# Running products of neighbouring groups made in shared steps, in a fused attention, MoE and FFN kernel

## The chip, the cores and the metric

The kernel runs on one core of one Trainium2 chip. The metric is the device time of one execution in microseconds (us). The kernel before took 1003.48 us (median of 3 runs, 1002.42 to 1005.08).

## The reference

Three stages follow one another; all data are float32, and the weights of the last stage come as float64 bits.

```python
# 1. attention with a decaying state: 4 batches x 8 heads, S = 768 steps, D = 48
a = a_re + i a_im, scaled by min(|a|, 0.999) / (|a| + 1e-6)
for t in range(S):
    state = a[t] * state + k[t] (x) v[t]      # complex, 48 x 48, a per row
    y[t]  = q[t] . Re(state)
# 2. mixture of 8 experts on 3072 tokens of 384 columns, one expert each
out[mask] = gate * (relu(x[mask] @ w1[e]) @ w2[e])
# 3. feed-forward: h = ((x @ w1) * (x @ w2)) @ w3 ; out = h @ w_out
```

## The kernel before

The 768 steps are cut into chunks of 64 steps, and four chunks of every batch and head make a group: three groups of 128 lanes by 64 steps. Within a chunk the recurrence is turned into matmuls by the running product P of the scaled a from the chunk's first step on: queries are multiplied by P, keys by its inverse.

**The elementwise stage** (`elementwise`, the first stream) makes 24 pieces of 8 steps, eight for each group, one group after the other. For a piece ScalarE (ACT) squares a and takes logarithm and exponential (`root`), and VectorE (DVE) scales (`norm`, L834 to L841) into a tile `cf` of coefficients, of which ACT copies one row negated (L842). `prefix` runs the complex product: each step is one multiply `pr<-cf,P` of 128x192 (L860) and one add `P<-pr` of 128x96 (L862), and each step needs the one before it. `power`, `weigh` and `keys` make the inverse weights, and the multiply `qk<-P,qkr` of 128x1536 (L892) makes a piece of weighted queries and keys, which a DMA stores to a DRAM tensor `qkd`. One call of `mix` weaves the steps of piece i with `keys` of piece i-2 and `norm` of piece i+1.

**The attention units** (`groups`, the second stream) wait until all eight pieces of their group are made. `ends` transposes the group's last products on TensorE (PE) and then, for groups 1 and 2, runs dense matmuls that nothing reads (`dense`, L964). Each group has eight units. A unit loads its keys and queries `kk` (L990, on SP's queue), turns them (`turn`, L974), makes scores, masks them on DVE (`at<-sc,mask`, L1006), makes outputs, and carries the state to the next chunk: `cb` or `cc` (L1074) and `W` or `ca` (L1075) on DVE, `L1073` on ACT. Outputs go on to the routing of the experts (rows L138 to L160).

**The product of w3 and w_out.** With the start of the third group, `side()` starts its steps: the loads `fdr` (L291, on SP), and `halves`, which turns float64 bits into pairs of float32 on DVE and ACT in 16 conversions: eight of 128x384 for w_out, eight of 128x512 for w3 (L322, L323, L324, L336, L337, L339). Once the third group's units are through, PE makes the first blocks `Wf` (L350 to L352), then the experts and the feed-forward stage run.

**What sets the order.** `drive` takes steps from the two streams by the costs that they yield; then a scheduler with a model of its own puts each engine's instructions in one fixed order. Each engine works through its list in that order, and waits where an instruction's inputs are not there.

Of the kernel before, what the change touches and what calls it, by code (L numbers as in the profile page):

```python
# [9 lines left out]
F32 = mybir.dt.float32  # L10
# [4 lines left out]
AF = mybir.ActivationFunctionType  # L15
# [607 lines left out]
D = 48  # L623
# [3 lines left out]
NPC = C // TP  # L627
NPIECE = NG * NPC
R2 = 2 * D
HD = NH * D  # L630
# [145 lines left out]
class Attn:  # L776
# [7 lines left out]
    def load_a(self, i):  # L784

        a = self.ep.tile([128, 2, 2, TP * D], F32, tag="a", name=f"a{i}", bufs=3)
        g, p = divmod(i, NPC)
        src = self.S.a[g].rearrange("r l (p e) -> p l r e", e=TP * D)
        if i:
            self.nc.sync.dma_start(a, src[p : p + 2].rearrange("n l r e -> l r n e"))  # L790
        else:
            for n in range(2):
                self.nc.sync.dma_start(a[:, :, n], src[n])
        return [a[:, :, n] for n in range(2)]

    def load_qk(self, i):
        g, p = divmod(i, NPC)
        x = self.e2.tile([128, TP, 2, D], F32, tag="qkr", name=f"qkr{i}", bufs=3)
        self.nc.sync.dma_start(x, self.S.qk[g, :, p * TP : (p + 1) * TP])
        return x  # L800

    def elementwise(self, aside, factors):
# [41 lines left out]

        def twice(c):

            p, r, d = (list(x) for x in c.ap)
            return bass.AP(tensor=c.tensor, offset=c.offset + r[0], ap=[p, [r[0], 2], [-r[0], 2], d])

        def prefix(i):  # L850
            p = i % NPC
            P[i] = e2.tile([128, TP, 2, D], F32, tag="P", name=f"P{i}", bufs=3)
            for t in range(TP):
                if p == 0 and t == 0:
                    v.tensor_copy(P[i][:, 0], cf[i][:, 0, 1:3])
                    yield 120
                    continue
                pv = P[i][:, t - 1] if t else P[i - 1][:, TP - 1]
                pr = e2.tile([128, 2, 2, D], F32, tag="pr", name=f"pr{i}_{t}", bufs=2)
                v.tensor_tensor(out=pr, in0=twice(cf[i][:, t]), in1=bc(pv, 2, 1), op=ALU.mult)  # L860
                yield 270
                v.tensor_tensor(out=P[i][:, t], in0=pr[:, :, 0], in1=pr[:, :, 1], op=ALU.add)  # L862
                yield 170

        def power(i):
            g, p = divmod(i, NPC)
            s2[i] = e2.tile([128, 2, E], F32, tag="s2", name=f"s2_{i}", bufs=2)
            act.activation(out=s2[i].rearrange("p r (t d) -> p t r d", d=D), in_=P[i], func=AF.Square)  # L868
            if p == NPC - 1:
                self.last[g] = l = self.st.tile([128, 2, 2, D], F32, tag="td", name=f"td{g}")  # L870
                act.copy(l, P[i][:, TP - 1].unsqueeze(2).to_broadcast([128, 2, 2, D]))

# [6 lines left out]
        def keys(i):  # L879
            g, p = divmod(i, NPC)  # L880
            k = raw[i][:, :, 1]
            x, g0 = s2[i][:, 0], s2[i][:, 1]
            if p == NPC - 1:
                v.tensor_copy(S.xm[:, g], px[i][:, E - D :])
            v.tensor_tensor(out=x, in0=px[i], in1=g0, op=ALU.mult)
# [7 lines left out]
            yield 1740  # L893
            dst = S.qkd[g].rearrange("q c h b (p t) w e -> p (q c h b) (t w e)", p=NPC)[p]
            self.stored = self.qk.pop(i).rearrange("p t w r d -> p (t w r d)")
            if p == NPC - 1:
                nc.sync.dma_start(dst[:64], self.stored[:64])
                done = nc.gpsimd.dma_start(dst[64:], self.stored[64:])
            else:
                done = nc.gpsimd.dma_start(dst, self.stored)  # L900
            with self.tc.issue_after(done.ins):
# [24 lines left out]
        for i in range(NPIECE + 1):  # L926
# [7 lines left out]
            if i + 1 < NPIECE:  # L934
                raw[i + 1] = self.load_qk(i + 1)
            ends = [j >= 0 and j % NPC == NPC - 1 for j in (i - 2, i - 1)]
            rest = [keys(i - 2)] if i > 1 and not ends[0] else []
# [169 lines left out]
    def groups(self, route, side, free):  # L1107
# [14 lines left out]
        yield lambda: self.made >= NPC  # L1122
# [3 lines left out]
        step = 0  # L1126
        for n, u in enumerate(work):
            g, q, c = u
            if q == 0 and c == 0:
                while self.pool and self.made < (g + 1) * NPC:  # L1130
                    yield self.fill(1)
                yield lambda: self.made >= (g + 1) * NPC
                yield from self.ends(g)
                for x in work[n : n + 2]:
                    ld[x] = self.loads(x)
                if g == NG - 1:
                    yield free
                    singles = side.fuse.units
                    side()
            self.pool.append(Item("scores", self.scores(u, ld[u][1])))  # L1140
            for x in self.chain(u, ld.pop(u)):
                yield x
                yield self.fill(S.fillcost)
                step += 1
                if g == NG - 1:
# [265 lines left out]
```

## Time and profile before

| | |
|---|---|
| median of 3 runs | 1003.48 us (1002.42 to 1005.08) |
| the profiled execution | 1001.18 us, its span 999.5 us |
| granted TensorE clock, mean over the span | 0.944 |
| busy over the span | PE 898.7 us (90%), DVE 609.1 (61%), ACT 487.3 (49%), POOL 130.9 (13%) |

The profile's page has the span in 40 slices of 25 us, a digit for the busy tenths of each, and below them the granted clock in tenths:

```profile
PE   3545899967997988999989999998999999999997
DVE  6999999997993885576489995442232323232222
PEclk9666999978997999899999999999999999999999
```

The elementwise stage is the run of nines of DVE in the slices 2 to 12. From the slice 18 on PE stands at 8 or 9 nearly throughout: there the experts and the feed-forward stage run.

### The profile page before, as it was taken

What the parts mean: (1) busy time and instruction counts of PE and PEld (TensorE: products, weight loads), DVE (VectorE), ACT (ScalarE), POOL (GpSimd) and SP (SyncE); (2) the same over time, 40 slices, a digit from 0 to 9 for tenths busy, and PEclk for the clock granted to TensorE, in tenths of its full rate; (3) what the DMA queues carried; (4) which work ended last, traced back from release to release, by engine and by line L of the source; (5) the groups of instructions that cost most, each with busy time, mean ns of one, the idle gap of its engine ahead of it and who ended that gap; (6) DMA issues with size and microseconds to landing.
All of it is one profiled execution on the core that took longest, in us unless ns stands there. A gap on an engine that the chain in (4) does not pass through costs nothing. (4 is left out here: it accounts for less than half of the span.)

```text
span 999.5 us, 17055 instructions
## 1 busy us (share of the span) xinstructions
PE 898.7 (90%) x6402; PEld 768.5 (77%) x6402; DVE 609.1 (61%) x1373; ACT 487.3 (49%) x1089; POOL 130.9 (13%) x197
## 2 busy tenths in 40 slices
PE   3545899967997988999989999998999999999997
PEld 1222478746886877989989999997888888888886
DVE  6999999997993885576489995442232323232222
ACT  6555688866774775444456654543231313121211
POOL 5111000211020211000232211110000000000001
PEclk9666999978997999899999999999999999999999
DMA  6566975448737763453677745630000000000000
GB/s 221 180 203 234 297 254 176 130 131 283 233 121 242 226 208 124 147 176 118 192 214 188 203 112 136 138 66 2 1 9 24 10 23 9 24 8 25 9 24 31
DMA packets 90183, 128.75 MB, mean 129 GB/s; under 512 B 7232, under 2 KB 72688, under 8 KB 90096
## 3 DMA queue, kind: packets, MB, share of 16 engines
q1 hardware_dynamic: 76300, 82.61, 28.9%
q0 software_dynamic: 10688, 40.36, 11.4%
q10 hardware_dynamic: 3108, 4.65, 1.7%
q8 instruction: 51, 0.84, 0.4%
q14 instruction: 36, 0.29, 0.1%
HBM read 92.38 MB, written 35.22 MB: 128 GB/s over the span
## 5 line engine op out<-in xcount | busy, mean ns | idle before, releaser
L606 DVE TENSOR_TENSOR ab<-asb,pb 128x512 f32<-128x512 f32 x48 | 33.0, 687 | 189.8 <-PE pb L352 184.2
L345 ACT CAST h<-w 128x384 fp32r<-128x384 f32 x128 | 65.1, 513 | 95.8 <-PE ph L351 50.9
L346 DVE TENSOR_TENSOR l<-w,h 128x384 fp32r<-128x384 f32 x128 | 70.6, 554 | 63.2 <-ACT h L345 60.6
L601 ACT COPY asb<-pa 128x512 f32<-128x512 f32 x48 | 28.2, 587 | 123.1 <-PE pa L352 117.0
L345 ACT CAST gh<-ab 128x512 fp32r<-128x512 f32 x48 | 29.7, 620 | 94.7 <-DVE ab L606 94.7
L816 PE MATMUL x<-s,ident 128*128 128x384 f32 x64 | 36.2, 703 | 43.5 <-ACT s L868 43.5
L351 PE MATMUL py<-hl,h 128*128 128x432 f32 x192 | 70.0, 365 | 3.5 <-DVE hl L407 3.5
L350 PE MATMUL py<-hh,h 128*128 128x432 f32 x192 | 69.2, 361 | 0.8 <-ACT hh L406 0.8
L350 PE MATMUL ph<-xh,h 128*128 128x432 f32 x192 | 69.7, 364 | 0.0
L352 PE MATMUL ph<-xh,l 128*128 128x432 f32 x192 | 69.6, 363 | 0.0
L351 PE MATMUL ph<-xl,h 128*128 128x432 f32 x192 | 69.6, 362 | 0.0
L352 PE MATMUL py<-hh,l 128*128 128x432 f32 x192 | 69.1, 360 | 0.0
L860 DVE TENSOR_TENSOR pr<-cf,P 128x192 f32<-128x192 f32 x189 | 66.6, 353 | 3.3
L974 PE MATMUL tr<-ident,kk 128*96 128x128 f32 x384 | 60.1, 289 | 9.1 <-DMA kk<-qkd 8.4
L351 PE MATMUL po<-ol,gh 128*128 128x384 f32 x192 | 65.0, 338 | 0.0
L350 PE MATMUL po<-oh,gh 128*128 128x384 f32 x192 | 64.8, 338 | 0.0
L352 PE MATMUL po<-oh,gl 128*128 128x384 f32 x192 | 64.2, 338 | 0.0
L570 POOL DMA_INDIRECT out<-ob,mdp x24 | 23.8, 992 | 307.6 <-DVE ob L569 165.8
L975 ACT COPY qkT<-tr 96x512 f32<-96x512 f32 x96 | 54.7, 591 | 18.2 <-PE tr L974 17.7
L350 PE MATMUL pa<-yh,ah 128*128 128x512 f32 x144 | 57.5, 399 | 3.0 <-ACT yh L345 3.0
L816 PEld LDWEIGHTS x<-s,ident 128*128 128x128 f32 x64 | 14.9, 258 | 56.7 <-ACT s L868 49.3
L350 PE MATMUL pb<-yh,bh 128*128 128x512 f32 x144 | 57.3, 398 | 0.0
(218 smaller groups left out, 2400.5 us busy)
## 6 DMA issues: line engine op xcount, KB each, us to landing
w<-in_w SPq DMA_DIRECT2D x128, 192.0 KB, 2.7
kk<-qkd SPq DMA_DIRECT2D x24, 768.0 KB, 9.7
qkd<-qk POOLq DMA_DIRECT2D x21, 768.0 KB, 5.7
qkr<-in_qk SPq DMA_DIRECT2D x24, 384.0 KB, 4.1
a<-in_a SPq DMA_DIRECT2D x11, 768.0 KB, 5.4
fdr<-in_w SPq DMA_DIRECT2D x16, 512.0 KB, 5.2
fdr<-in_v POOLq DMA_DIRECT2D x12, 512.0 KB, 6.5
xs<-zr POOLq DMA_DIRECT2D x8, 648.0 KB, 7.6
```

The lines of the kernel that those rows point to most:

```text
L345: nc.scalar.copy(H, src)
L346: nc.vector.tensor_tensor(out=L, in0=src, in1=H.bitcast(F32), op=ALU.subtract)
L350: nc.tensor.matmul(out, lh, rh, start=first, stop=False)
L351: nc.tensor.matmul(out, lh, rl, start=False, stop=False)
L352: return nc.tensor.matmul(out, ll, rh, start=False, stop=last)
L570: nc.gpsimd.indirect_dma_start(out=S.outv[j], out_offset=bass.IndirectOffsetOnAxis(ap=S.mdp[:, j, 0:1], axis=0), in_=ob, in_offset=None, b ...
L601: nc.scalar.copy(asb, pa)
L606: nc.vector.tensor_tensor(out=ab, in0=asb, in1=pb, op=ALU.mult)
L816: nc.tensor.matmul(p, S.ident, s[r], start=r == 0, stop=r == 1)
L860: v.tensor_tensor(out=pr, in0=twice(cf[i][:, t]), in1=bc(pv, 2, 1), op=ALU.mult)
L974: nc.tensor.transpose(pt[:, h], qk[:, h0 + h, w], self.S.ident)
L975: nc.scalar.copy(qkT[:, w, h0 : h0 + 4], pt)
```

## The change

The 24 pieces are made in 24 rounds of a new table `PAIRS`: four rounds of eight steps of group 1, eight rounds that take four steps of group 1 and four of group 2, eight rounds of groups 2 and 3 in the same way, and four rounds of group 3. In a shared round one multiply of 128x384 (L891 of the changed kernel) and one add of 128x192 (L893) make a step of both groups. `LAST` says after which round a group is complete: rounds 12, 20 and 24 instead of 8, 16 and 24. `cf` has a fourth row, which ACT copies. Loads of a and of queries and keys, and the stores, go in two parts in a shared round. `ends` calls `dense` for the first group alone. The next group's first `kk` are loaded as soon as that group is made, and `side()` starts as soon as the elementwise stage has been issued.

```diff
+HEAD = 4
+def rounds():
+    got = [((0, TP * r, TP),) for r in range(HEAD)]
+    for g in range(NG - 1):
+        more = C - HEAD * TP
+        got += [((g, HEAD * TP + t, TP // 2), (g + 1, t, TP // 2)) for t in range(0, more, TP // 2)]
+        got += [((g + 1, t, TP),) for t in range(more, C if g == NG - 2 else HEAD * TP, TP)]
+    return got
+PAIRS = rounds()
+LAST = {g: max(r for r, x in enumerate(PAIRS) if g in [y[0] for y in x]) for g in range(NG)}
...
-            cf[i] = c = ep.tile([128, TP, 3, D], F32, tag="cf", name=f"cf{i}", bufs=2)
+            cf[i] = c = ep.tile([128, TP, 4, D], F32, tag="cf", name=f"cf{i}", bufs=2)
-            v.tensor_tensor(out=c[:, :, 1:3], in0=ar, in1=bc(td(u), 2, 2), op=ALU.mult)
-            act.activation(out=c[:, :, 0], in_=c[:, :, 2], func=AF.Copy, scale=-1.0)
+            v.tensor_tensor(out=c[:, :, 0:3:2], in0=ar, in1=bc(td(u), 2, 2), op=ALU.mult)
+            act.activation(out=c[:, :, 1], in_=c[:, :, 2], func=AF.Copy, scale=-1.0)
+            act.copy(c[:, :, 3], c[:, :, 0])
...
-                v.tensor_tensor(out=pr, in0=twice(cf[i][:, t]), in1=bc(pv, 2, 1), op=ALU.mult)
-                yield 270
-                v.tensor_tensor(out=P[i][:, t], in0=pr[:, :, 0], in1=pr[:, :, 1], op=ALU.add)
-                yield 170
+                pr = e2.tile([128, 2, 2, 2, D], F32, tag="pr", name=f"pr{i}_{t}", bufs=1)[:, :j]
+                cx = c[:, :j, t].rearrange("p m (w r) d -> p m w r d", w=2)
+                v.tensor_tensor(out=pr, in0=cx, in1=bc(pv, 2, 2), op=ALU.mult)
+                yield 100 + 170 * j
+                v.tensor_tensor(out=o[:, :j, t], in0=pr[:, :, :, 0], in1=pr[:, :, :, 1], op=ALU.add)
+                yield 70 + 100 * j
...
-        if g < NG - 1:
+        if not g:
             self.dense(self.stored[:, :512], WARM)
...
-                    ld[x] = self.loads(x)
+                    if x not in ld:
+                        ld[x] = self.loads(x)
                 if g == NG - 1:
                     yield free
-                    singles = side.fuse.units
-                    side()
+            if free() and not singles:
+                singles = side.fuse.units
+                side()
...
-                if x[0] == g and x not in ld:
+                if self.made > LAST[x[0]] and x not in ld:
                     ld[x] = self.loads(x)
```

DVE in the fifth piece, before: the steps of group 1's running product, one multiply and one add each (L837 belongs to the next piece).

```order
L860 TENSOR_TENSOR pr_0_420<-cf_384,P_362 128x192
L837 SCALAR_TENSOR_TENSOR sq_351<-sq_351,y_356 128x384
L862 TENSOR_TENSOR P_419<-pr_0_420 128x96
L860 TENSOR_TENSOR pr_1_425<-cf_384,P_419 128x192
L862 TENSOR_TENSOR P_419<-pr_1_425 128x96
L860 TENSOR_TENSOR pr_2_431<-cf_384,P_419 128x192
L862 TENSOR_TENSOR P_419<-pr_2_431 128x96
L860 TENSOR_TENSOR pr_3_439<-cf_384,P_419 128x192
L862 TENSOR_TENSOR P_419<-pr_3_439 128x96
```

The same place on DVE in the changed kernel, the first shared round (its first step is group 1's alone, as group 2's first product is a copy; L860 is here the line that was L837):

```order
L891 TENSOR_TENSOR pr_0_438<-cf_398,P_376 128x192
L893 TENSOR_TENSOR P_435<-pr_0_438 128x96
L891 TENSOR_TENSOR pr_1_443<-cf_398,P_435 128x384
L893 TENSOR_TENSOR P_435<-pr_1_443 128x2x96
L891 TENSOR_TENSOR pr_2_452<-cf_398,P_435 128x384
L860 SCALAR_TENSOR_TENSOR sq_364<-sq_364,y_369 128x384
L893 TENSOR_TENSOR P_435<-pr_2_452 128x2x96
L891 TENSOR_TENSOR pr_3_460<-cf_398,P_435 128x384
L893 TENSOR_TENSOR P_435<-pr_3_460 128x2x96
```

Where eight narrow steps stood for one group, four of twice the width stand for two groups; 62 steps are of this kind.

DVE at the end of the elementwise stage, before: the last `qk` multiply, the state of group 2's last chunk (`cc`, `ca`), then the first conversion.

```order
L892 TENSOR_TENSOR qk_3533<-P_3294,qkr_3142 128x1536
L1074 TENSOR_TENSOR cc_183<-W,T_2150 96x384
L1075 TENSOR_TENSOR ca_182<-W,T_2150 96x768
L336 TENSOR_SCALAR fdm<-fdr 128x384
L337 TENSOR_SCALAR fdl<-fdr 128x384
L138 TENSOR_REDUCE mx<-lg 128x4
L339 SCALAR_TENSOR_TENSOR fdr<-fdr,fdl 128x384
```

The same place in the changed kernel, in which L923 is the `qk` multiply, L1041 the mask, L1109 and L1110 the state:

```order
L1041 TENSOR_TENSOR at_2607<-sc_2590,mask 128x512
L916 TENSOR_TENSOR s_23_2758<-s_23_2758 128x384
L918 TENSOR_TENSOR qkr_2414<-qkr_2414,s_23_2758 128x8x48
L920 SCALAR_TENSOR_TENSOR qkr_2414<-s_23_2758,qkr_2414 128x8x48
L923 TENSOR_TENSOR qk_2836<-P_2617,qkr_2414 128x1536
L1109 TENSOR_TENSOR cb_2634<-W,T_2251 96x384
L1110 TENSOR_TENSOR W<-W,T_2251 96x2x384
L1041 TENSOR_TENSOR at_2749<-sc_2732,mask 128x512
L336 TENSOR_SCALAR fdm<-fdr 128x384
L337 TENSOR_SCALAR fdl<-fdr 128x384
L339 SCALAR_TENSOR_TENSOR fdr<-fdr,fdl 128x384
```

The last `qk` multiply now has 11 of the masks of the groups 1 and 2 ahead of it instead of all 16, and the conversions begin beside group 2's fourth unit.

DVE at group 3's first mask, before (`at_3615`), which stands among the first conversions of w_out:

```order
L323 TENSOR_SCALAR fdm<-woh 128x384
L145 TENSOR_TENSOR oh_3499<-key_3492,kx_3497 128x32
L337 TENSOR_SCALAR fdl<-fdr 128x384
L324 SCALAR_TENSOR_TENSOR wol<-fdr,fdm 128x384
L160 TENSOR_TENSOR run<-run,oh_3499 128x8
L1006 TENSOR_TENSOR at_3615<-sc_3598,mask 128x512
L339 SCALAR_TENSOR_TENSOR fdr<-fdr,fdl 128x384
L1074 TENSOR_TENSOR cb_3649<-W,T_3545 96x384
```

The same mask in the changed kernel (`at_3596`), among the last conversions of w3:

```order
L1109 TENSOR_TENSOR cc_186<-W,T_2251 96x384
L1110 TENSOR_TENSOR ca_185<-W,T_2251 96x768
L324 SCALAR_TENSOR_TENSOR w3l_3762<-fdr,fdm 128x512
L322 TENSOR_TENSOR w3h_3761<-fdr,fdm 128x512
L336 TENSOR_SCALAR fdm<-fdr 128x512
L323 TENSOR_SCALAR fdm<-w3h_3761 128x512
L1041 TENSOR_TENSOR at_3596<-sc_3579,mask 128x512
L324 SCALAR_TENSOR_TENSOR w3l_3762<-fdr,fdm 128x512
L322 TENSOR_TENSOR w3h_3918<-fdr,fdm 128x512
```

Between the last `qk` multiply and group 3's first mask stand 88 of the 96 conversion instructions, four masks, five pairs of state instructions and 13 short rows of routing; before, ten conversion instructions stood there, and the others lay between the units of group 3.

## Rows read from the trace of the kernel before

**Rows 1.** Timeline of DVE: start, duration, instruction (steps of the running product).

```profile
107.62 0.36 DVE L860 TENSOR_TENSOR pr<-cf,P 128x192 f32<-128x192 f32 x1
108.01 0.26 DVE L862 TENSOR_TENSOR P<-pr 128x96 f32<-128x96 f32 x1
108.30 0.36 DVE L860 TENSOR_TENSOR pr<-cf,P 128x192 f32<-128x192 f32 x1
```

**Rows 2.** Groups of DVE by form, 0 to 305 us: busy us, mean ns | idle before.

```profile
L860 DVE TENSOR_TENSOR pr<-cf,P 128x192 f32<-128x192 f32 x189 | 66.6, 353 | 3.3
L862 DVE TENSOR_TENSOR P<-pr 128x96 f32<-128x96 f32 x189 | 47.9, 253 | 3.2
...
L834 DVE SCALAR_TENSOR_TENSOR sq<-sq,y 128x384 f32<-128x384 f32 x24 | 13.2, 549 | 0.0
L1075 DVE TENSOR_TENSOR W<-W,T 96x768 f32<-96x768 f32 x12 | 11.5, 954 | 0.0
L1006 DVE TENSOR_TENSOR at<-sc,mask 128x512 f32<-128x512 f32 x16 | 10.9, 684 | 0.9 <-PE sc L1002 0.8
```

**Rows 3.** Timeline of DVE at four places; in brackets the idle time before.

```profile
237.65 0.55 DVE L1074 TENSOR_TENSOR cb<-W,T 96x384 f32<-96x384 f32 x1 [6.69 <-ACT cb L1073]
...
303.37 1.76 DVE L892 TENSOR_TENSOR qk<-P,qkr 128x1536 f32<-128x1536 f32 x1
...
321.04 0.36 DVE L336 TENSOR_SCALAR fdm<-fdr 128x384 int32<-128x384 int32 x1 [9.63 <-DMA fdr<-in_w_out]
...
326.13 0.68 DVE L1006 TENSOR_TENSOR at<-sc,mask 128x512 f32<-128x512 f32 x1
```

**Rows 4.** Timeline of DVE: group 2's first and last mask, group 3's last.

```profile
240.16 0.69 DVE L1006 TENSOR_TENSOR at<-sc,mask 128x512 f32<-128x512 f32 x1
...
295.96 0.68 DVE L1006 TENSOR_TENSOR at<-sc,mask 128x512 f32<-128x512 f32 x1
296.56 0.24 DVE L862 TENSOR_TENSOR P<-pr 128x96 f32<-128x96 f32 x1
...
391.55 0.68 DVE L1006 TENSOR_TENSOR at<-sc,mask 128x512 f32<-128x512 f32 x1
```

**Rows 5.** Timeline of PE: the first matmul of the product of w3 and w_out.

```profile
405.57 0.69 PE L350 MATMUL Wf<-woh,w3h 128*128 128x384 f32 x1
```

**Rows 6.** Groups of ACT by form, 0 to 305 us.

```profile
L842 ACT ACTIVATE cf<-cf 128x384 f32<-128x384 f32 x24 | 12.7, 529 | 0.3
```

**Rows 7.** Timeline of SP: DMA issues.

```profile
308.99 2.53 SPq L990 DMA_DIRECT2D kk<-qkd  x3
311.69 4.62 SPq L291 DMA_DIRECT2D fdr<-in_w_out  x5
```

**Rows 8.** DMA issues, 300 to 400 us: KB each, median us to landing.

```profile
fdr<-in_w_out SPq DMA_DIRECT2D x8, 384.0 KB, 5.8
```

**Rows 9.** Waits of DVE, 100 to 410 us: us in total, times, longest.

```profile
DVE fdl L337 <- DMA fdr<-in_w: 7.9, 5, 3.7
```

**Rows 10.** Groups of DVE by line, 321 to 385 us: the conversions, and one row of routing.

```profile
L339 DVE SCALAR_TENSOR_TENSOR fdr<-fdr,fdl 128x384 f32<-128x384 uint32 (+1 forms) x16 | 9.8, 614 | 0.0
L337 DVE TENSOR_SCALAR fdl<-fdr 128x384 uint16<-128x384 uint16 (+1 forms) x16 | 6.4, 400 | 8.0 <-DMA fdr<-in_w 7.9
L336 DVE TENSOR_SCALAR fdm<-fdr 128x384 int32<-128x384 int32 (+1 forms) x16 | 6.1, 388 | 9.6 <-DMA fdr<-in_w_out 9.6
L322 DVE TENSOR_TENSOR w3h<-fdr,fdm 128x512 fp32r<-128x512 f32 x8 | 5.5, 683 | 0.0
L324 DVE SCALAR_TENSOR_TENSOR w3l<-fdr,fdm 128x512 fp32r<-128x512 f32 x8 | 5.4, 686 | 0.0
...
L324 DVE SCALAR_TENSOR_TENSOR wol<-fdr,fdm 128x384 fp32r<-128x384 f32 x8 | 4.4, 548 | 0.0
L322 DVE TENSOR_TENSOR woh<-fdr,fdm 128x384 fp32r<-128x384 f32 x8 | 4.4, 547 | 0.0
...
L323 DVE TENSOR_SCALAR fdm<-w3h 128x512 int32<-128x512 int32 x8 | 3.3, 420 | 0.0
L323 DVE TENSOR_SCALAR fdm<-woh 128x384 int32<-128x384 int32 x8 | 2.8, 355 | 0.0
...
L160 DVE TENSOR_TENSOR run<-run,oh 128x8 f32<-128x8 f32 x8 | 1.3, 158 | 0.1
```

**Rows 11.** Stretches of 25 us: busy of PE, PEld, DVE, ACT, POOL; granted clock; DMA share.

```profile
150.00:175.00 25.00, 25.00 (x330) 21.31 (x329) 23.61 (x56) 21.83 (x64) 1.06 (x2) 1.00 0.57 176
200.00:225.00 25.00, 16.84 (x94) 10.34 (x91) 24.66 (x70) 15.13 (x34) 4.07 (x5) 0.73 0.42 132
300.00:325.00 25.00, 19.79 (x180) 16.28 (x177) 9.47 (x24) 11.28 (x33) 0.57 (x1) 0.73 0.78 244
```

More of the change, by code (lines that the diff above doesn't have):

```diff
@@ L786, in load_a @@
         a = self.ep.tile([128, 2, 2, TP * D], F32, tag="a", name=f"a{i}", bufs=3)
[L787 to L794, printed above, removed]
+        at = 0
+        for g, t, n in PAIRS[i]:
+            src = self.S.a[g][:, :, t * D : (t + 2 * n) * D].rearrange("r l (m e) -> m l r e", m=2)
+            dst = a[:, :, :, at : at + n * D]
+            if i and n == TP:
+                self.nc.sync.dma_start(a, src.rearrange("m l r e -> l r m e"))
+            elif i:
+                for r in range(2):
+                    self.nc.sync.dma_start(dst[:, r], src[:, :, r].rearrange("m l e -> l m e"))
+            else:
+                for m in range(2):
+                    self.nc.sync.dma_start(dst[:, :, m], src[m])
+            at += n * D
+        return [a[:, :, m] for m in range(2)]
     def load_qk(self, i):
-        g, p = divmod(i, NPC)
         x = self.e2.tile([128, TP, 2, D], F32, tag="qkr", name=f"qkr{i}", bufs=3)
-        self.nc.sync.dma_start(x, self.S.qk[g, :, p * TP : (p + 1) * TP])
+        at = 0
+        for g, t, n in PAIRS[i]:
+            self.nc.sync.dma_start(x[:, at : at + n], self.S.qk[g, :, t : t + n])
+            at += n
         return x
@@ L843, in norm @@
+            act.activation(out=c[:, :, 1], in_=c[:, :, 2], func=AF.Copy, scale=-1.0)
+            act.copy(c[:, :, 3], c[:, :, 0])
             yield 870
-        def twice(c):
-            p, r, d = (list(x) for x in c.ap)
-            return bass.AP(tensor=c.tensor, offset=c.offset + r[0], ap=[p, [r[0], 2], [-r[0], 2], d])
         def prefix(i):
-            p = i % NPC
             P[i] = e2.tile([128, TP, 2, D], F32, tag="P", name=f"P{i}", bufs=3)
[L853 to L856, printed above, removed]
-                    continue
-                pv = P[i][:, t - 1] if t else P[i - 1][:, TP - 1]
-                pr = e2.tile([128, 2, 2, D], F32, tag="pr", name=f"pr{i}_{t}", bufs=2)
-                v.tensor_tensor(out=pr, in0=twice(cf[i][:, t]), in1=bc(pv, 2, 1), op=ALU.mult)
-                yield 270
-                v.tensor_tensor(out=P[i][:, t], in0=pr[:, :, 0], in1=pr[:, :, 1], op=ALU.add)
-                yield 170
+            m = len(PAIRS[i])
@@ new lines, in prefix @@
+            n = TP // m
+            run = lambda x: x.rearrange("p (m t) r d -> p m t r d", m=m)
+            c, o = run(cf[i]), run(P[i])
+            for t in range(n):
+                k = [k for k in range(m) if t or PAIRS[i][k][1]]
+                for x in range(m):
+                    if x not in k:
+                        v.tensor_copy(o[:, x, 0], c[:, x, 0, 0:3:2])
+                        yield 120
+                if not k:
+                    continue
+                if t:
+                    pv = o[:, :, t - 1]
+                else:
+                    old = len(PAIRS[i - 1])
+                    pv = P[i - 1].rearrange("p (m t) r d -> p m t r d", m=old)[:, old - len(k) :, TP // old - 1]
+                j = len(k)
+                pr = e2.tile([128, 2, 2, 2, D], F32, tag="pr", name=f"pr{i}_{t}", bufs=1)[:, :j]
[4 more added lines that the diff above has]
+                yield 70 + 100 * j
@@ L865, in power @@
         def power(i):
-            g, p = divmod(i, NPC)
             s2[i] = e2.tile([128, 2, E], F32, tag="s2", name=f"s2_{i}", bufs=2)
             act.activation(out=s2[i].rearrange("p r (t d) -> p t r d", d=D), in_=P[i], func=AF.Square)
-            if p == NPC - 1:
+            g, _, n = PAIRS[i][0]
+            if i == LAST[g]:
                 self.last[g] = l = self.st.tile([128, 2, 2, D], F32, tag="td", name=f"td{g}")
-                act.copy(l, P[i][:, TP - 1].unsqueeze(2).to_broadcast([128, 2, 2, D]))
+                act.copy(l, P[i][:, n - 1].unsqueeze(2).to_broadcast([128, 2, 2, D]))
@@ L893, in keys @@
             yield 1740
-            dst = S.qkd[g].rearrange("q c h b (p t) w e -> p (q c h b) (t w e)", p=NPC)[p]
             self.stored = self.qk.pop(i).rearrange("p t w r d -> p (t w r d)")
[L896 to L900, printed above, removed]
+            at = 0
+            for g, t, n in PAIRS[i]:
+                dst = S.qkd[g].rearrange("q c h b t w e -> (q c h b) t (w e)")[:, t : t + n].rearrange("l t e -> l (t e)")
+                src = self.stored[:, at * 2 * R2 : (at + n) * 2 * R2]
+                if i == LAST[g]:
+                    nc.sync.dma_start(dst[:64], src[:64])
+                    done = nc.gpsimd.dma_start(dst[64:], src[64:])
+                else:
+                    done = nc.gpsimd.dma_start(dst, src)
+                at += n
             with self.tc.issue_after(done.ins):
@@ L935, in elementwise @@
                 raw[i + 1] = self.load_qk(i + 1)
-            ends = [j >= 0 and j % NPC == NPC - 1 for j in (i - 2, i - 1)]
+            ends = [j in LAST.values() for j in (i - 2, i - 1)]
             rest = [keys(i - 2)] if i > 1 and not ends[0] else []
@@ L1126, in groups @@
         step = 0
+        singles = None
         for n, u in enumerate(work):
@@ L1144, in groups @@
                 step += 1
-                if g == NG - 1:
+                if singles:
                     for _ in range(1 + (step % 3 == 0)):
```

12 lines of the change are left out of this document (6 added, 6 removed).

## The prediction

> **What bounds the kernel now.** I read the strips of the page first. From 425 us on PE is the bound (its digits stand at 8 or 9), and the change touches nothing there; so the question is when the first matmul of the w3 and w_out product starts, 405.57 us before [rows 5]. Ahead of it I read the stretches, DVE's groups and its timeline. To 305 us DVE is full wherever the attention doesn't hold it (24.66 of 25 us at 200 to 225) [rows 11], and the running product is its largest part: 66.6 us of multiplies and 47.9 of adds [rows 2]. Its last multiply for `qkd` starts at 303.37 and ends at 305.13, and the first conversion only starts at 321.04, after 9.63 us of waiting for its load [rows 3]. PE has holes meanwhile: 16.84 busy of 25 us at 200 to 225 and 19.79 at 300 to 325, with a granted clock of 0.73 in both, between its levels of 1.2 and 2.4 GHz, against 1.00 at 150 to 175 where it is full [rows 11]. So three legs set the 405.57: DVE's elementwise work to 305, the gap and start of group 3 to its first mask at 326.13 [rows 3], and group 3, of which the last mask is at 391.55 [rows 4] and the product 14.0 us later.
>
> **The end of the elementwise work.** 62 steps now serve two groups. A 128x384 multiply costs 549 ns, as L834 does, and a 128x192 add 353, as the old multiply [rows 2]. By durations a step of two groups falls from 2 x (353 + 253) = 1212 to 902 ns; 62 of them save 19.2 us. Two bounds lie around it. Chained, with nothing between, a narrow step took 108.30 - 107.62 = 0.68 us, 0.04 more than one duration at each of its two instructions [rows 1]; a wide one would take 0.97, and 62 x (1.36 - 0.97) = 24.2. With other work between, an instruction starts about 0.08 us before its forerunner's end (the mask of 0.68 at 295.96, the add at 296.56 [rows 4]); that takes four such overlaps off 1212 and two off 902, and 62 x 0.14 = 8.7 remain. The order shows both kinds; I take 17, nearer to the durations.
>
> The Trainium skill, "VectorE: DVE Perf Modes", section "The DRAIN you can't avoid", says that the next instruction does not start until the pipe is empty. By that alone the saving would be the 19.2 of the durations; [rows 4] show a start 0.08 us ahead of the end, so the measurement decides, and the sum would move by 2 us only.
>
> Five attention units fewer stand ahead of the last `qk` multiply (11 masks in place of 16, by the order): a mask of 684, a state pair of 954 and 0.55 [rows 2, 3], less three overlaps of 0.08, make 1.93 each, 9.6 us. They are moved, not removed. The wait of 6.69 for group 2's first `cb` [rows 3], which was group 2's start in the middle of the elementwise work, has group 2 ready only at round 20 now and DVE filled with other steps; I take it as gone (bounds 0 and 6.7). 13 short routing rows at 0.158 [rows 10], with their overlaps 1.7 us in my estimate, move behind it too. So 305.1 - 17 - 9.6 - 6.7 - 1.7 = 270.1 us (262.9 with the saving at 24.2, 278.4 at 8.7).
>
> ACT gets 24 more copies of about 529 ns [rows 6], 12.7 us. In its fullest stretch it is busy for 21.83 of 25 us [rows 11]; with 12.7 us more over some 265 it rises by 1.2 a stretch, to 92%. I cost the copy at nothing: it is hidden by DVE as long as ACT is under full. Without that cover it is late for the next round's steps, at up to 0.5 us a round, 12 us.
>
> The split loads and stores cost issue time on SP and POOL alone. The dense matmuls ahead of group 2 ran in a stretch in which PE waited anyway (200 to 225 [rows 11]); without them the clock may be at 0.73 for longer at that start, but the mask rate decides below, not this start.
>
> **The gap and the conversions.** Before, the first `fdr` load was issued at 311.69, 6.6 us after the `qk` multiply's end, of which 2.53 went into issuing three loads of group 3's keys [rows 7], which aren't ahead of it now. I take 6.6 - 2.5 = 4.1 us to the issue and 5.8 to the landing [rows 8], 9.9 (bounds: 8, and the 15.9 from 305.13 to 321.04 as before [rows 3]). DVE starts to convert at 280.0.
>
> Now comes the cost. All conversions are 48.1 us of DVE (nine rows of [rows 10]: 9.8 + 6.4 + 6.1 + 5.5 + 5.4 + 4.4 + 4.4 + 3.3 + 2.8). Before, they lay among group 3's units; now 88 of 96 stand ahead of group 3's first mask. The eight left out are of the wide kind, about 0.53 each, so 43.8, less 88 overlaps of 0.08, 36.8. With four masks at 0.60 (2.4), five state pairs at 1.34 (6.7) and 13 short rows (1.3) that is 47.2 us back to back. Waits for loads come on top: 7.9 us before [rows 9], 6 taken here, since the loads have more time to run ahead (bounds 0 and 7.9). Group 3's first mask: 280.0 + 47.2 + 6 = 333.2, against 326.13 before.
>
> Group 2's five last units need 5 x 7.97 = 40 us from the last `qk` multiply on, by the pace of its masks ((295.96 - 240.16) / 7 = 7.97 [rows 4]), so PE would be ready at 318; DVE's list is what is late.
>
> **Group 3 without conversions.** Before, its eight masks took 391.55 - 326.13 = 65.4 us; group 2's took 55.8 [rows 3, 4]. I take group 2's pace, which had DVE full with other work, and the 14.0 to the product as before: 69.8 (bounds: 64, if the pace is PE's alone at about 7.1, and 79.4 as before). So the product starts at 333.2 + 69.8 = 403.0 against 405.57: 2.6 us earlier, and the rest stands as it was. From the profiled 1001.18 that is 998.6. The median of the runs lies 2.3 above the profiled execution, so 1000.9.
>
> **The rivals.**
> 1. Conversions don't hold group 3 back. They do less than I say if the steps are mostly chained (saving 24.2, end at 262.9), the load comes in 8 us and none after it is waited for: 262.9 + 8 + 47.2 = 318.1, then 69.8, product at 387.9, 17.7 us earlier. For it: every PE hole of [rows 11] disappears with the group starts. Against it: 47 us of DVE in one piece can't be shorter. Centre 12 us faster, 991 by the runs; from 5 to 22.
> 2. Slower: DVE's list between the last `qk` multiply and group 3's first mask. Its price is one us for each us that this mask comes after 405.57 - 69.8 = 335.8, and it decides from there, 2.6 us later than I forecast. With the saving at 8.7 or ACT as the bound (278.4), the load as before (15.9), waits of 7.9 and group 3's old pace: 278.4 + 15.9 + 47.2 + 7.9 + 79.4 = 428.8, 23 slower; centre 10 slower, 1013.5. For it: 88 instructions moved ahead of that mask, and each wait for a load now stops the attention too. Against it: all four bounds would have to fall on the bad side for the whole.
> 3. Small loads late: two loads of a pair become four, with rows half as long. 16 rounds held up by 1 us each would make 16 us at the elementwise end, 1015. Against it: DVE's largest waits of that time are not for loads of a, and these are issued two rounds ahead.
>
> The Trainium skill, "DMA: Bandwidth & Descriptors", section "Rules for kernel authors", wants many small transfers coalesced into one large one, which speaks against the split. No run here shows the split yet; it is what the third rival would be by that page.
>
> **How the numbers follow.** Forecast 0.46 (995 to 1007 by itself), first rival 0.27, second 0.24, third 0.03. Within 0.3%, about what a measurement of this kernel tells from no change, means 1000.5 to 1006.5. The forecast gives 0.21 faster, 0.20 same, 0.05 slower; the first rival 0.25 and 0.02 same; the second 0.03 same and 0.21 slower; the third 0.03 slower. Together 0.46, 0.25, 0.29. The range runs from 987 to 1015, which leaves the outer third of either rival out.
>
> **What would show it.** Right: multiplies of 128x384 in the steps at about 0.55 us, the last `qk` multiply ending near 270, the first conversion near 280 after a wait for `fdr`, group 3's first mask near 333 with almost no conversion after it, its masks 8 us apart, the product at 403. Wrong: a first mask at 318 or earlier (rival 1) or past 336 (rival 2), a wait of DVE for ACT's copy in the steps, ACT near full at 125 to 270, waits for a or `qkr` (rival 3), or a later part of the span that isn't the same length.

## The result and the profile after

The changed kernel took 1013.28 us (median of 4 runs, 1012.64 to 1014.76) against 1004.07 before: 1.0109 times the time before, 95% interval 1.0092 to 1.0126. It is slower, where 1000.9 us was forecast; the range of 987 to 1015 holds the time, but the sign is the second rival's. The same kernel beside the experiments gave 1.0108 (1.0075 to 1.0142). In the two profiled executions the product of w3 and w_out starts 11.4 us later (405.57 before, 416.95 now), and what follows it takes 597.8 us in place of 595.6; the account below is of the 11.4.

The steps first. In the groups of DVE to 275 us (busy us, mean ns), these answer to [rows 2]; 62 wide steps, at the durations that were taken for them:

```profile
L891 DVE TENSOR_TENSOR pr<-cf,P 128x384 f32<-128x384 f32 x62 | 34.2, 552 | 0.7
L891 DVE TENSOR_TENSOR pr<-cf,P 128x192 f32<-128x192 f32 x65 | 22.9, 353 | 1.0
L893 DVE TENSOR_TENSOR P<-pr 128x192 f32<-128x192 f32 x62 | 21.8, 352 | 0.8
```

DVE's timeline (start, duration, instruction, idle time before it) from the last `qk` multiply to group 3's last mask, with [rows 3, 4] as its counterpart:

```profile
268.58 1.76 DVE L923 TENSOR_TENSOR qk<-P,qkr 128x1536 f32<-128x1536 f32 x1
...
275.15 0.69 DVE L1041 TENSOR_TENSOR at<-sc,mask 128x512 f32<-128x512 f32 x1 [2.84 <-PE sc L1037]
280.60 0.36 DVE L336 TENSOR_SCALAR fdm<-fdr 128x384 int32<-128x384 int32 x1 [4.76 <-DMA fdr<-in_w_out]
...
282.83 0.36 DVE L336 TENSOR_SCALAR fdm<-fdr 128x384 int32<-128x384 int32 x1 [1.00 <-DMA fdr<-in_w_out]
...
284.85 0.55 DVE L1109 TENSOR_TENSOR cc<-W,T 96x384 f32<-96x384 f32 x1
...
340.00 0.68 DVE L1041 TENSOR_TENSOR at<-sc,mask 128x512 f32<-128x512 f32 x1
...
398.14 0.69 DVE L1041 TENSOR_TENSOR at<-sc,mask 128x512 f32<-128x512 f32 x1 [4.34 <-PE y L1057]
```

The elementwise stage ends at 270.3 (forecast 270.1) and the first conversion starts at 280.60 (280.0). Then it goes apart: group 3's first mask at 340.00 (333.2). The state `cc` at 284.85 stands behind nine conversion instructions, of which the first waited 4.76 us for its load and the fourth 1.00. PE's first product matmul, 405.57 before [rows 5], is at

```profile
416.95 0.69 PE L350 MATMUL Wf<-woh,w3h 128*128 128x384 f32 x1
```

ACT's timeline at the same place: the conversions have instructions there too, and the first of them waits for DVE's conversion, with group 2's state and an output copy in line behind it.

```profile
281.00 0.61 ACT L329 ACTIVATE fdm<-fdm,rebias 128x384 int32<-128x384 int32 x1 [4.22 <-DVE fdm L336]
281.55 0.55 ACT L330 ACTIVATE fdr<-fdr 128x384 f32<-128x384 f32 x1
282.00 1.60 ACT L1108 ACTIVATE cc<-W,T 96x48 f32<-96x48 f32 x8
...
284.42 0.48 ACT L1060 COPY xo<-y 128x384 f32<-128x384 f32 x1
```

And PE, which waits for that copy for 3.95 us:

```profile
284.95 0.90 PE L123 MATMUL rt<-ident,xo 128*128 128x128 f32 x3 [3.95 <-ACT xo L1060]
```

The same happens once more, without ACT between: a conversion waits 1.85 us for a load of w3, group 2's state `W` stands next but one behind it, and PE, which needs `W`, has waited 4.49 us when it gets it.

```profile
325.98 0.43 DVE L337 TENSOR_SCALAR fdl<-fdr 128x512 uint16<-128x512 uint16 x1 [1.85 <-DMA fdr<-in_w]
...
326.93 0.95 DVE L1110 TENSOR_TENSOR W<-W,T 96x768 f32<-96x768 f32 x1
```

```profile
327.94 2.87 PE L1094 MATMUL W<-cb,perm 96*96 96x384 f32 x4 [4.49 <-DVE W L1110]
```

At the other end of the attention, its beginning, I had not looked. Group 1's first mask, before and after:

```profile
123.81 0.68 DVE L1006 TENSOR_TENSOR at<-sc,mask 128x512 f32<-128x512 f32 x1
```

```profile
154.64 0.69 DVE L1041 TENSOR_TENSOR at<-sc,mask 128x512 f32<-128x512 f32 x1
```

Group 1 is complete after round 12 instead of 8, so the attention starts 30.8 us later. By group 2's first mask 8.3 of these are left (240.16 before [rows 4]):

```profile
248.43 0.68 DVE L1041 TENSOR_TENSOR at<-sc,mask 128x512 f32<-128x512 f32 x1
```

From there to group 3's first mask it takes 91.6 us (248.43 to 340.00), 86.0 before (240.16 to 326.13).

What PE does from its first `kk` transpose to the first product matmul, before and after (length, then busy PE, PEld, DVE, ACT, POOL; clock, DMA share, GB/s):

```profile
114.81:405.57 290.76, 259.56 (x3393) 211.81 (x3394) 236.49 (x600) 204.22 (x529) 36.07 (x38) 0.93 0.61 195
```

```profile
142.92:416.95 274.03, 245.13 (x3347) 204.14 (x3346) 194.22 (x457) 188.54 (x490) 33.67 (x40) 0.91 0.58 184
```

PE is busy for 89% of either stretch. It starts 28.1 us later and is through in 16.7 us less. Of PE's busy time 21.2 us are no longer in the stretch (11.7 of adds of the elementwise stage, most of which now lie ahead of it, and 9.5 of dense matmuls, with each matmul counted from the end of the one before it). But the other 3329 matmuls, the same in both, take 6.8 us more, 239.7 against 232.9, and only 2.3 us of idle time are saved (31.2 before, 28.9 after). So 28.1 - 21.2 + 6.8 - 2.3 = 11.4 us is the loss, 405.57 to 416.95. Where the holes of PE are, in stretches of the changed kernel:

```profile
175.00:200.00 25.00, 18.97 (x170) 16.08 (x171) 24.25 (x47) 19.50 (x48) 3.21 (x6) 0.68 0.51 170
200.00:225.00 25.00, 24.49 (x375) 21.36 (x375) 21.62 (x56) 20.62 (x59) 2.16 (x4) 0.98 0.45 134
...
275.00:300.00 25.00, 21.05 (x257) 18.59 (x255) 15.33 (x44) 14.47 (x40) 0.00 (x0) 0.73 0.58 179
300.00:325.00 25.00, 21.59 (x333) 18.34 (x327) 20.76 (x51) 19.33 (x48) 5.51 (x4) 0.98 0.84 272
325.00:350.00 25.00, 22.00 (x290) 18.40 (x291) 21.70 (x51) 16.85 (x42) 0.00 (x0) 0.81 0.67 204
350.00:375.00 25.00, 25.00 (x376) 20.42 (x376) 6.04 (x16) 15.48 (x39) 5.84 (x6) 1.00 0.56 181
```

The hole at 200 to 225 of [rows 11] is closed, and one of 6.0 us stands at 175 to 200, in group 1. In the conversions, at 275 to 350, there are 10.4 us of holes; the granted clock, whose two levels are 1.2 and 2.4 GHz (1.00 is the upper), averages 0.73, 0.98 and 0.81 there. From 350 to 375 PE is full and DVE is idle three quarters of the time, and the last mask before the product waits for PE (398.14 above).

### The profile page after: what moved, and what is told of

Its sections match the earlier page's. It is cut to its first block, busy times and chain, and to the rows that moved or that the text cites. A ratio compares the mean times of both kernels' runs of the same rounds, so it can differ in the third digit from the quotient of the medians.

```text
span 1012.6 us, 17062 instructions
## 1 busy us (share of the span) xinstructions
PE 899.2 (89%) x6386; PEld 765.8 (76%) x6386; DVE 597.4 (59%) x1249; ACT 499.9 (49%) x1113; POOL 136.6 (13%) x213
## 5 line engine op out<-in xcount | busy, mean ns | idle before, releaser
L1010 ACT COPY qkT<-tr 96x512 f32<-96x512 f32 x96 | 54.7, 597 | 16.4 <-PE tr L1009 15.9
L891 DVE TENSOR_TENSOR pr<-cf,P 128x192 f32<-128x192 f32 (+1 forms) x127 | 57.1, 450 | 1.7
L351 PE MATMUL pb<-yl,bh 128*128 128x512 f32 x144 | 56.9, 395 | 0.0
```

Source lines behind the costliest of these rows:

```text
L351: nc.tensor.matmul(out, lh, rl, start=False, stop=False)
L891: v.tensor_tensor(out=pr, in0=cx, in1=bc(pv, 2, 2), op=ALU.mult)
L1010: nc.scalar.copy(qkT[:, w, h0 : h0 + 4], pt)
```

## The experiments

Three theories. A: PE is nearly full from the attention's start to the product, so the start 30 us later is what costs. B: the conversions, in DVE's list ahead of group 2's and 3's attention, cost it. C: the small edits do. Each ratio is to the kernel before on the same chip, with its 95% interval.

| run | ratio | group 1's / 3's first mask, product, us |
|---|---|---|
| head8 | 1.0009 (0.9984 to 1.0034) | 123.3 / 338.3 / 415.8 |
| head6 | 1.0014 (0.9985 to 1.0042) | 137.0 / 324.7 / 407.1 |
| narrow | 1.0079 (1.0055 to 1.0103) | 156.3 / 342.1 / 421.8 |
| held | 1.0041 (1.0018 to 1.0064) | 154.6 / 327.6 / 416.4 |
| after_again | 1.0108 (1.0075 to 1.0142) | 154.6 / 344.8 / 424.2 |
| late_start | 1.0077 (1.0050 to 1.0103) | 148.9 / 337.8 / 421.0 |
| spread | 0.9957 (0.9927 to 0.9988) | 154.6 / 329.7 / 405.9 |
| head6_spread | 1.0002 (0.9974 to 1.0030) | 138.2 / 324.1 / 411.3 |
| paced | 0.9925 (0.9901 to 0.9950) | 154.7 / 320.8 / 395.9 |
| before_spread | 0.9989 (0.9966 to 1.0012) | 125.2 / 327.8 / 404.3 |
| spread_dense | 0.9988 (0.9954 to 1.0023) | 154.9 / 330.8 / 407.9 |
| spread_slow | 0.9963 (0.9948 to 0.9979) | 154.6 / 323.1 / 400.4 |
| hold_once | 1.0019 (0.9999 to 1.0039) | 155.6 / 332.9 / 411.6 |
| before_paced | 0.9968 (0.9942 to 0.9995) | 123.8 / 327.9 / 402.5 |
| head6_paced | 0.9992 (0.9971 to 1.0014) | 137.2 / 322.0 / 408.4 |

The times in us are of one profiled execution each, the ratios of all runs; where the two differ (head8's execution was one of its longest, 1014.66 us at a clock of 0.93), the ratio decides. The chips differ too: the kernel before took 1009.78 us beside the first four runs of the table, 1009.15 beside the next four, 1003.04 and 1004.15 beside the rest. So points late in the span are compared within such a group: the changed kernel itself has its product at 416.95 in the section above and at 424.2 in the second group.

**head8**: no round is shared.

```diff
-HEAD = 4
+HEAD = 8
```

> HEAD at 8: no round is shared, the groups are complete after rounds 8, 16 and 24 as before, and the conversions start behind the whole elementwise stage at group 3's start as before; the fourth row of cf with its copy on ACT, the early loads of kk and the missing dense matmuls of group 2 stay in. Theory A (late start: the attention is bound by PE and the change begins it 30 us later, first mask 154.6 in place of 123.8): first mask back at about 124, time about 1004, within 3. Theory B (conversions ahead of group 3's first mask hold it to 340): that mask back at about 326, also about 1004. Theory C (the small edits cost it: the copy, the missing dense matmuls, the early kk): stays at 1009 or more.

C falls: the copy, the early `kk` and the missing dense matmuls together cost 0.1%, no more than 0.34%. Nothing is said yet between A and B.

**head6**: half the sharing.

```diff
-HEAD = 4
+HEAD = 6
```

> HEAD at 6: 31 shared double steps in place of 62, groups complete after rounds 10, 18 and 24. Theory A: group 1 starts about 15 us earlier than in the changed kernel (first mask near 139), and PE, bound, hands 5 to 10 us of that on: about 1005. Theory B: the elementwise stage ends some 8 us later (278) and with it the conversions and group 3's first mask (345): 1017 or more. Theory C: 1013 as it stands.

The time is theory A's: group 1 starts 17.6 us earlier than in the changed kernel, and the loss is gone. But it doesn't speak against B as I had expected, because the edit takes the conversions out of the way as well: the elementwise stage ends later (last `qk` multiply at 290.35), and only 32 of the conversion instructions stand ahead of group 3's first mask, in place of 88 (21 in head8). And between head8 (1.0009) and head6 (1.0014) nothing of DVE's saving reaches the time.

**narrow**: a shared step in two multiplies and two adds.

```diff
-                v.tensor_tensor(out=pr, in0=cx, in1=bc(pv, 2, 2), op=ALU.mult)
-                v.tensor_tensor(out=o[:, :j, t], in0=pr[:, :, :, 0], in1=pr[:, :, :, 1], op=ALU.add)
+                for x in range(j):
+                    v.tensor_tensor(out=pr[:, x], in0=cx[:, x], in1=bc(pv[:, x], 2, 1), op=ALU.mult)
+                    v.tensor_tensor(out=o[:, x, t], in0=pr[:, x, :, 0], in1=pr[:, x, :, 1], op=ALU.add)
```

> The rounds and their order as in the changed kernel, but each shared step made by two multiplies of 128x192 and two adds of 128x96. This prices the wide steps: I took 17 us (bounds 8.7 and 24.2) for 62, so the last qk multiply should end at 287 in place of 270.3. Theory A: half of the shared steps of the first eight rounds come ahead of group 1's start, so that is 4 us later, and the time 1018 to 1024. Theory B: the conversions start 17 us later, and all of it comes through: 1030.

Its last `qk` multiply, on DVE's timeline:

```profile
277.51 1.75 DVE L924 TENSOR_TENSOR qk<-P,qkr 128x1536 f32<-128x1536 f32 x1
```

8.9 us later than in the changed kernel, and 5.5 later than in held (272.04), which has the same wide steps and ran beside it; not 17. The narrow steps of the two groups alternate, so that each has another instruction between it and the one that it needs:

```profile
130.24 0.63 DVE L892 TENSOR_TENSOR pr<-cf,P 128x192 f32<-128x192 f32 x2
130.78 0.42 DVE L894 TENSOR_TENSOR P<-pr 128x96 f32<-128x96 f32 x2
131.12 0.95 DVE L864 TENSOR_TENSOR cf<-a,sq 128x768 f32<-128x768 f32 x1
```

Two steps take 0.88 us here, from 130.24 to 131.12, against 2 x 0.68 for chained ones [rows 1]. Summed over the elementwise stage, from the start of each step instruction to the start of the next instruction (waits over 0.15 us left out), the steps take 109.2 us before, 95.4 in narrow and 89.6 in the changed kernel: 13.8 of the 19.6 us come from the alternation, 5.8 from the width. Both expectations, 1018 us or more against 1004, were missed: in the ratio narrow can't be told from the changed kernel.

**held**: the conversions begin with group 3, each behind the latest mask in DVE's list.

```diff
+                    S.mark = nc.vector.tensor_tensor(out=at, in0=sc, in1=bc(S.mask, NH, 1), op=ALU.mult)
-        ... halves(S, nc, raws, wp, first), lambda: [S.end]
+        ... halves(S, nc, raws, wp, first), lambda: [S.end, S.mark]
-            if free() and not singles:
+            if g == NG - 1 and not singles:
```

> The conversions begin at group 3's first unit again, and each is kept behind the latest mask in the list, so that DVE cannot take them ahead; all else as in the changed kernel. Theory B: group 3's first mask falls from 340 to 315 to 320, group 3 then takes 65 us with the conversions in it as before, product at about 397 to 400 in place of 417: about 995 to 998. Theory A: PE is the bound from the first mask on and the mask order gives at most its few holes back: 1008 to 1013. Theory C: 1013.

Group 3's first mask came 12.4 us earlier, but the product at 416.4: group 3 took 72 us with all conversions in it, 58 without. The ratio lies at the near end of what theory A gave (1008 us is 1.004); the mask moved nearly as B had it and the product did not. Moving the whole lump is not the way out.

**after_again**: the changed kernel unchanged.

> The changed kernel once more, as the measure for the runs beside it: 1.011 times the kernel before, the product of w3 and w_out starting near 417.

Ratio as on record, product at 424.2 in that execution.

**late_start**: the kernel before, group 1 begun after twelve pieces.

```diff
-        yield lambda: self.made >= NPC
+        yield lambda: self.made >= NPC + 4
+                    with nullcontext() if any(u) else self.tc.issue_after(S.end.ins):
-                    nc.vector.tensor_tensor(out=at, in0=sc, in1=bc(S.mask, NH, 1), op=ALU.mult)
+                        nc.vector.tensor_tensor(out=at, in0=sc, in1=bc(S.mask, NH, 1), op=ALU.mult)
...
+        with nullcontext() if any(u) else self.tc.issue_after(S.end.ins):
+            ... (the state's two instructions of the first unit)
```

> The kernel before, without any part of the change, but with group 1's attention kept until twelve pieces are made in place of eight: its first mask and first state stand behind the twelfth qk multiply on DVE. Theory A (PE is nearly full from the attention's first matmul to the product, so a late start comes through): first mask near 150 in place of 123.8; PE's 231 us of attention work and some 25 to 30 us of holes follow, less 8 us of adds that lie ahead of the start now; product 5 to 15 us later, ratio 1.005 to 1.015. Theory B (what costs is the conversions ahead of group 3's first mask): they stand where they stood, the early holes of PE close instead, ratio 1.000 within 0.003.

This was meant to show theory A by itself, a late start without any other part of the change. The kernel is 0.8% slower, and the product is at

```profile
420.98 0.69 PE L350 MATMUL Wf<-woh,w3h 128*128 128x384 f32 x1
```

But theory B is in this run too. In the kernel before all masks of group 2 are through ahead of the first conversion; here group 2's last mask stands behind two conversion instructions, the first of which waits 8.97 us for its load, and PE waits for that mask:

```profile
324.52 0.36 DVE L336 TENSOR_SCALAR fdm<-fdr 128x384 int32<-128x384 int32 x1 [8.97 <-DMA fdr<-in_w_out]
324.80 0.35 DVE L337 TENSOR_SCALAR fdl<-fdr 128x384 uint16<-128x384 uint16 x1
325.07 0.68 DVE L1007 TENSOR_TENSOR at<-sc,mask 128x512 f32<-128x512 f32 x1
```

```profile
325.81 0.34 PE L1023 MATMUL y<-vz,at 128*64 128x48 f32 x1 [4.46 <-DVE at L1007]
```

That hole alone is 4.46 us, and 0.8% is about 8. So this run does not show the price of the late start by itself.

**spread**: the conversions early as in the change, two in an attention unit (the changed kernel has 2.67), each behind the latest mask (`S.mark` as in held).

```diff
-                    for _ in range(1 + (step % 3 == 0)):
+                    for _ in range(1):
```

> The changed kernel with the conversions begun early as there, but two for each unit in place of 2.67, and each behind the latest mask. Theory B: DVE has 5.4 us of conversions and 2.2 of masks and state in a unit, under PE's 8, so group 3's first mask falls to 320 to 328 and the product to 400 to 408: ratio about 1.000. Theory A: PE's work from the start on is the same, only holes of 5 us or so close: 1.004 to 1.010.

As theory B had it: with the same late start the product is at 405.9 (424.2 in the changed kernel beside it) and the kernel 0.4% faster than before. So whatever the late start costs can be made up, if the conversions don't stand in the way.

**head6_spread**: both edits.

> Rounds shared from the seventh on (groups complete after rounds 10, 18 and 24) together with the paced conversions. Theory A: the start is 13 us later than before instead of 28, and the group starts' holes are partly gone: product at 400 to 406, ratio 0.995 to 1.000. Theory B: first mask of group 3 near 320, ratio 0.990.

A miss: with half of the sharing, and group 1 starting 16.4 us earlier, nothing came on top; it is rather slower than spread, with intervals that overlap a little.

**paced**: the changed kernel with the mark alone (held's edits to `S.mark`); the rate stays 2.67 in a unit.

> The changed kernel with each conversion behind the latest mask, at the old rate of 2.67 for each unit (the kernel with two for each unit came to 0.996 of the time before). If it is the bulk, that is, that DVE takes conversions ahead of masks that it has the chance to serve first: as good as with two, 0.994 to 1.000. If it is the rate (2.67 conversions of 2.7 us, masks and state are 9.4 us of DVE in a unit, over PE's 8): 1.003 to 1.008, in between.

A little better than the first way of seeing it: 0.9925, the fastest here. The edit does nothing but tie the conversions' place in DVE's list, so that place is what costs the changed kernel its time, and the higher rate costs nothing against spread. Its DVE timeline where the changed kernel waited:

```profile
275.53 0.55 DVE L1109 TENSOR_TENSOR cc<-W,T 96x384 f32<-96x384 f32 x1 [3.31 <-ACT cc L1108]
...
279.01 0.69 DVE L1041 TENSOR_TENSOR at<-sc,mask 128x512 f32<-128x512 f32 x1 [1.24 <-PE sc L1037]
279.62 0.35 DVE L336 TENSOR_SCALAR fdm<-fdr 128x384 int32<-128x384 int32 x1
```

The first conversion starts 1 us earlier than in the changed kernel, without a wait, and `cc` 9.3 us earlier. From the first conversion to group 3's first mask (columns as before), the changed kernel and then paced:

```profile
280.60:340.00 59.40, 49.04 (x613) 41.23 (x610) 48.17 (x118) 41.71 (x106) 5.51 (x4) 0.80 0.68 220
```

```profile
279.60:320.80 41.20, 40.37 (x591) 33.86 (x590) 33.53 (x87) 33.05 (x87) 4.21 (x4) 1.00 0.77 250
```

PE has 10.4 us of holes and a clock of 0.80 in the one, 0.8 us and 1.00 in the other. Group 1 starts as late as in the changed kernel (154.7), and group 2's first mask is still 4.7 us later than before, but group 3's, at 320.75, is 5.4 earlier:

```profile
244.81 0.68 DVE L1041 TENSOR_TENSOR at<-sc,mask 128x512 f32<-128x512 f32 x1
```

**before_spread**: the kernel before with marks and two conversions in a unit.

> The kernel before with conversions paced in the same way, two for each unit and behind the latest mask. If pacing is worth 1.5% by itself, as between the changed kernel and its paced version: 0.985 to 0.992. If it only takes away what the change had added, because before the conversions lay among group 3's units anyway: 0.998 to 1.004, and then the shared steps are worth 0.4% with pacing.

Pacing is worth nothing measurable there at two in a unit.

**spread_dense**: spread, with the dense matmuls of group 2.

```diff
-        if not g:
+        if g < NG - 1:
             self.dense(self.stored[:, :512], WARM)
```

> The paced kernel (two for each unit) with the dense matmuls ahead of group 2 put back. Granted clock 0.64 at 175 to 200 us without them. If the clock is what they gave: faster by 2 to 4 us, 0.992 to 0.994. If they only take PE's time, since group 1's units run into group 2's start now: 7 to 9 us slower, 1.003 to 1.005.

0.3% slower than spread, with intervals that overlap: no gain from them here, and no measured loss.

**spread_slow**: 1.33 conversions in a unit.

```diff
-                    for _ in range(1):
+                    for _ in range(step % 3 > 0):
```

> The paced kernel with 1.33 conversions for each unit, which ends with the last unit instead of three units ahead of it. If DVE still holds the units back at two for each unit: 3 to 6 us faster, 0.990 to 0.993. If PE is the bound there already: the same product start, or later by the conversions that are left, 0.996 to 1.004.

No difference to spread that can be measured: the rate is not what counts.

**hold_once**: all early conversions behind one mask, the one at hand when they begin (`S.mark` is set as in held).

```diff
                 singles = side.fuse.units
+                S.hold = S.mark
-        ... lambda: [S.end, S.mark]
+        ... lambda: [S.end, S.hold]
```

> The changed kernel with all early conversions kept behind one mask only, that of group 2's fifth unit, where the first loads have landed; from there on DVE may take them as early as in the changed kernel, and 15 of 16 still stand ahead of group 3's first mask. If the wait for loads at the head of the lists is what costs: near the paced kernel, 0.993 to 0.998. If it is the bulk of conversion work ahead of the masks: near the changed kernel, 1.006 to 1.011.

In between: 1.0019. Its waits on DVE and PE at 270 to 345 us (total, times, longest):

```profile
DVE fdl L337 <- DMA fdr<-in_w: 7.1, 4, 2.5
```

```profile
PE tr L1009 <- ACT qkT L1010: 3.2, 1, 3.2
PE rt L123 <- ACT xo L1060: 3.1, 2, 1.9
```

The first wait is gone, later ones for w3 are still there, with the attention behind them. PE waits 7.3 us in all in this stretch, 10.3 in the changed kernel and 1.3 in paced, where DVE has no wait for a load. So by the ratios about half of the 1.8% between the changed kernel and paced goes with the first wait, by PE's waits in one execution of each a third, and the rest with the conversions that stand in line later.

**before_paced** and **head6_paced**: the mark alone, in the kernel before and with HEAD at 6.

> The kernel before with each conversion behind the latest mask, at its own rate. If the shared rounds are worth what the pair with two conversions for each unit showed (0.9989 without, 0.9957 with): 0.996 to 1.000 here against 0.9925. If pacing alone does it: 0.990 to 0.994.

> Paced as in the best kernel, with rounds shared from the seventh on, so that group 1 starts 15 us earlier and DVE saves half as much. If the earlier start counts (theory A): 0.988 to 0.992. If the elementwise stage's end and the conversions' start count: 0.995 to 1.000.

0.9968 without shared rounds, 0.9992 with half of them, 0.9925 with all. before_paced is as expected if the shared rounds are worth something beside the pacing; 0.4% by the middle values, with intervals that overlap a little, so their worth is not shown beyond doubt. None and half can't be told apart.

head6_paced came out as the second of its two expectations had it, against theory A: the earlier start gave nothing. Its trace shows why it lags behind paced. The conversions start at 306.37 in place of 279.62, and the tie to the latest mask didn't keep a late load from standing ahead of the next one. DVE, ACT and PE:

```profile
306.37 0.36 DVE L336 TENSOR_SCALAR fdm<-fdr 128x384 int32<-128x384 int32 x1 [5.67 <-DMA fdr<-in_w_out]
...
307.95 0.68 DVE L1041 TENSOR_TENSOR at<-sc,mask 128x512 f32<-128x512 f32 x1
```

```profile
306.76 0.61 ACT L329 ACTIVATE fdm<-fdm,rebias 128x384 int32<-128x384 int32 x1 [6.73 <-DVE fdm L336]
```

```profile
308.84 1.09 PE L1009 MATMUL tr<-ident,kk 128*96 128x128 f32 x4 [5.03 <-ACT qkT L1010]
```

From the first `kk` to the product ACT waits 12.0 us for DVE's part of conversions there, 2.5 in paced, and PE has 29.3 us of holes, 16.8 in paced; the product is 12.5 us later.

## Why the prediction was wrong

- **The end of the elementwise work** (270.1): 270.3, right to 0.2 us by luck. The terms are 19.6 us for the steps (17 forecast; the durations alone gave 19.2), 9.6 for the moved units (9.6), 5.6 of waits (6.7) and 0.6 of routing (1.7), less 0.5 that the rest of the stage takes longer; and in other executions with the same elementwise stage the end lies from 266.7 (paced) to 273.9 (after_again). Of the steps' saving the larger part is the alternation of two groups, which the sum didn't tell from the width. Its bounds have slips: 62 x 0.15 is 9.3 and not 8.7, and with 0.98 for a chained wide step 24.2 becomes 23.6.
- **ACT's copy at nothing**: right. It cost 506 ns a round of ACT, and head8 shows no loss from it.
- **The first conversion at 280.0**: right, 280.60.
- **The step that failed: "conversions 47.2 us back to back, waits for loads 6, first mask at 333.2"**. The work was near, 48.17 us of DVE; the idle time was 11.2 us instead of 6. Waits for loads made 7.3 of it after the first conversion, and 3.7 were waits for ACT, which I hadn't counted: 1.1 for ACT's share of a conversion, 1.7 and 0.9 for a copy of routing and one of the state that stand in ACT's list with such shares. ACT waited for DVE's conversions in turn (4.22 us at 281.00), so a late load stops two engines, and PE behind them. First conversion 0.6, work 1.0 and idle time 5.2 later than forecast make 6.8 us. paced, which changes only the conversions' place, shows that this step lost the time: there DVE waits for no load at all, and group 3's first mask is at 320.75.
- **Group 3's pace and the 14.0 us to the product**: 58.1 instead of 55.8, and 18.8 instead of 14.0. I took group 2's pace for one that DVE set; but PE is full in both stretches, and after the last mask it has 14.84 us of work in place of 9.71. First the kernel before, then the changed one:

```profile
240.16:295.96 55.80, 55.80 (x882) 48.62 (x881) 54.15 (x140) 43.15 (x113) 6.52 (x8) 1.00 0.53 171
391.55:405.57 14.02, 9.71 (x138) 7.77 (x135) 2.71 (x7) 3.26 (x11) 1.94 (x2) 0.79 0.07 29
```

```profile
340.00:398.14 58.14, 58.14 (x889) 49.08 (x888) 21.68 (x61) 35.57 (x93) 7.79 (x8) 1.00 0.41 129
398.14:416.95 18.81, 14.84 (x177) 11.67 (x177) 3.93 (x13) 5.19 (x15) 1.94 (x2) 0.80 0.05 22
```

6.8 + 2.3 + 4.8 makes 13.9 of the 13.95 us between the forecast 403.0 and 416.95.

- **What the sum left out: group 1's start.** It followed DVE's leg alone, and took PE's readiness "at 318" for certain, though its addends give 310 (270.1 + 40). paced came near it with nothing in the way (320.75). The 30.8 us by which the attention begins later were nowhere in the sum. What they cost stays open: 8.3 us were left of them at group 2's first mask, late_start's 0.8% has a conversion's wait in it, paced and spread start as late and are faster than the kernel before, and head6_paced starts earlier and is not measurably faster.
- **The second rival** named the place and the mechanism (a load waited for in DVE's list stops the attention) and the point of 335.8; it got 0.24. The first (conversions that don't hold group 3) did not come in this kernel; paced comes close to it, with the product at 395.9, 9.7 us earlier than before. The third did not happen: no wait for `a` or `qkr` shows in the changed kernel's waits from 100 us on.

## What to carry to other kernels

When side work is moved forward in an in-order list, ask what waits at its head and what stands behind it, on every engine that has a share of it. Tying each piece to the instruction that it must not overtake turned 1.1% of loss into 0.75% of gain here without moving a step of the computation. The tie isn't enough by itself: in head6_paced a late load still stood ahead of a mask, so look at when the first load lands as well. And where one engine is busy nine tenths of a stretch, follow its list too, from its first instruction to its last: a sum along another engine's list leaves out what the busy one has left to do.

## What was not expected of the hardware

Alternating two independent chains of 192- and 96-column instructions on DVE gave more than half of what joining them into instructions of twice the width gave in all: the steps' summed time was 109.2 us before, 95.4 with narrow steps in shared rounds and 89.6 with wide ones.

Holes of PE went with more than their length. The 3329 matmuls of the attention and its routing, the same in all three kernels, kept PE busy for 232.9 us before, 239.7 in the changed kernel and 230.7 in paced, with a granted clock of 0.93, 0.91 and 0.96 over the stretch and 31.2, 28.9 and 16.9 us of holes in it. But the clock did not fall with every idle time: stretches of 25 us had 0.73 with 3.95 us of idle time, 0.81 with 3.0, and 0.98 with 3.41. The two low ones hold the ends of single holes of 3.95 and 4.49 us (284.95 and 327.94 above).
